# A Trainium2 transformer block: three of four row blocks turned by DMA, residual sums shared by VectorE and GpSimd, a small product moved to VectorE, and a new order

## The chip, the cores and the metric

One Trainium2 core runs the whole program. TensorE (PE) multiplies, VectorE (DVE), ScalarE (ACT) and GpSimd (POOL) do the elementwise work, and SyncE (SP) issues every DMA transfer, one after the other in a written order. The metric is the device time of one execution in microseconds; lower is better. Before the change it is 191.43 us, the median of three runs (191.26 to 191.53).

## What is computed

```python
def _A_ref(x, wqkv, wo):                  # B, S, D = 1, 2048, 448; H = 16 heads of 28
    qkv = (x @ wqkv).reshape(B, S, 3, H, Dh) ...
    off = jnp.arange(8) * 2               # each row looks at itself and 7 rows before it, two apart
    logits = jnp.einsum("bhsd,bhswd->bhsw", q, kg) * scale
    attn = _softmax(jnp.where(mask, logits, -1e9))
    o = jnp.einsum("bhsw,bhswd->bhsd", attn, vg)
    return o...reshape(B, S, D) @ wo

def _B_ref(x, w1, w2, w3, w4):
    h = _gelu(_layernorm(x) @ w1)         # 448 to 448
    hs = concat(four groups of 112 channels, shifted by 1, -1, 2, -2 rows) @ w2
    x1 = x + hs
    return x1 + _gelu(_layernorm(x1) @ w3) @ w4     # 448 to 1792 to 448

h  = x + _A_ref(_layernorm(x), wqkv, wo)
h2 = h + _B_ref(_layernorm(h), w1, w2, w3, w4)
```

Inputs, weights and output are bfloat16.

## The kernel before

The 2048 rows stand in 16 tiles of 128 rows (`xin`), four tiles to a block. Blocks t = 0 to 3 go through these phases: N1 (statistics and normalise into `lntm`), A1 (turn the normalised rows so that features lie on partitions, `actT`, then q and k), V, A2 (scores: products `qk_r` of q with eight shifted copies of k on VectorE, summed over a head's features on TensorE with the 0/1 matrix `zc`), S (softmax: `mx`, `ls`, `pb`, turned on TensorE to `pt`), A3 (`bd_r`: probabilities spread into block-diagonal form on VectorE, then multiplied with `vw`, the windowed values), O (the product with `wo_s`, and the residual sum into `xin`), B1 and M (norm, turn, w1 and gelu into `gT`). The second half runs in five units of 2, 4, 4, 4 and 2 tiles: B2 (w2, then `xb` = residual + product, f32), T (norm of `xb`, and the outer residual `xb += xin`), W3 (gelu into `h3T`), B3 (w4, the last sum into `ost`, and the store). In the profile the large buffers share one allocation and show as `arena`: an `arena<-arena,xin` row on 128x448 f32 is the outer residual sum `xb += xin`; `arena<-xin,rs_y,ps` is the eviction of w2 into `xb`; `lntm<-arena,...` the norm of unit T.

Every operation is recorded first by `_Sched.add` or `group`, with its reads and writes, and given a number. The engines' programs are then cut from one list, `ORDER` (line 22 on): each engine runs its operations in the order in which their numbers stand there, and so does SP with its transfers. Buffers are handed out in that order too (`arrange`), and semaphore waits are derived from it (`_emit_plan`). Nothing is decided while the kernel runs. An operation that may run on either of two engines has an alternative in `alts`; the numbers in `OTHER` (line 53) take it. All operations are issued from one line of `emit_engine`, 1011 before and 1012 after, so the rows of the profile are told apart by the names of their tiles; line 1006 is a load of ScalarE's function table.

`TURN` (line 13) says for each block and phase how `transposed` turns the normalised rows: `t` by TensorE transposes and two copies out of PSUM, `d` by one DMA transpose that SP issues. Block 0 of A1 with `t` takes `transposed_single`. For `d`, `normalize` writes 512 columns per tile (two overlapping pieces of 256) in place of 448. The matmuls of this kernel contract 64 rows at a time, so that two run beside each other in the two halves of TensorE (`duo`); that is why rows read `64*128 64x448`.

`rstd` computes the reciprocal deviation; for the norm B1 (kind 1) it also makes `mrs`, the mean times the reciprocal deviation, that the last sum in B3 adds. `phase_B2` issues the 16 outer residual sums on GpSimd.

Of the kernel before, what the change touches and what calls it, by code (L numbers as in the profile page):

```python
# [6 lines left out]
ALU = mybir.AluOpType  # L7
# [2 lines left out]
F32 = mybir.dt.float32  # L10

_LAST = {}
TURN = {'A1': 'ttdd', 'B1': 'dddd', 'B2': 'ddddd'}
NORM = {'N0': 'vvvv', 'N1': 'avvv', 'B1': 'avvv', 'B2': 'avvvv'}
STATS = {'N1': 'vvva', 'B1': 'avaa', 'B2': 'avvvv'}
NBD, NLN, NACT, NSM, NO = 3, 2, 4, 1, 5
# [3 lines left out]
STAGE = '....'  # L20
ALONE = False
ORDER = """
# [29 lines left out]
"""  # L52
OTHER = """
91 94 114 187 188 501 507 549 550
"""
FULL = (4,)
FILL = (1, 1, 0, 0)
# [228 lines left out]
def bass_sequential_preLN__sliding_local_dilated__mixer_s_mlp__prompt_kernel(  # L286
# [16 lines left out]
    S = _Sched()  # L303
# [16 lines left out]
    with ExitStack() as es:  # L320
# [3 lines left out]
        xin = sb("xin", [128, NTL, D], BF16)  # L324
# [17 lines left out]
        rs_y = sb("rs_y", [128, 3, 2, NTL], F32)  # L342
        mrs = sb("mrs", [128, NTL], F32)
        nm = sb("nm", [128, 3, NTL], F32)
# [35 lines left out]
        xb = [arv(A_KV + i // 4 * KVB, 128, 4 * D * 2).bitcast(F32).rearrange("p (i d) -> p i d", d=D)[:, i % 4, :] for i in range(NTL)]  # L380
# [28 lines left out]
        def dve(meth, block=False, **kw):  # L409
            op = S.add("dve", meth, **kw)  # L410
            op.block = block
            return op

        def pool(meth, **kw):
            return S.add("pool", meth, **kw)
# [90 lines left out]
        def rstd(kind, i, m=4, summed=False, norms="v", how="p"):  # L506
            var = mv[:, kind, i:i + m, 1]
            by = 1.0 / D if summed else 1.0
            first = int(kind == 1)
            shifted_ = "a" in norms  # L510

            def power(k):
                S.add("pool", "tensor_tensor", out=rs_y[:, kind, k, i:i + m], in0=rs_x[:, kind, k, i:i + m], in1=mhalf[:, 0:m], op=ALU.pow)

            def power_act(k):
                act(rs_x[:, kind, k, i:i + m], var, ACT.Ln, scale=by * (1.0 + EPS * k), bias=epsilon[:, k:k + 1])
                act(rs_y[:, kind, k, i:i + m], rs_x[:, kind, k, i:i + m], ACT.Exp, scale=-0.5)

            def shift(k):
                if m == 1:  # L520
                    act(nmr[:, kind, i:i + 1], nm[:, kind, i:i + 1], ACT.Identity, scale=rs_y[:, kind, k, i:i + 1])
                else:
                    dve("tensor_tensor", out=nmr[:, kind, i:i + m], in0=nm[:, kind, i:i + m], in1=rs_y[:, kind, k, i:i + m], op=ALU.mult)

            if not summed and (shifted_ or kind == 1):
                dve("tensor_scalar", out=nm[:, kind, i:i + m], in0=mv[:, kind, i:i + m, 0], scalar1=-1.0, scalar2=None, op0=ALU.mult)
            if how == "a":
                power_act(first)
                if shifted_:
                    shift(first)  # L530
                if kind == 1:
                    power_act(0)
            else:
                if kind == 1:
                    dve("tensor_scalar", out=rs_x[:, kind, 1, i:i + m], in0=var, scalar1=by * (1.0 + EPS), scalar2=EPS * EPS, op0=ALU.mult, op1=ALU.add)
                    power(1)
                    if shifted_:
                        shift(1)
                if kind == 1 or summed:
                    dve("tensor_scalar", out=rs_x[:, kind, 0, i:i + m], in0=var, scalar1=by, scalar2=EPS, op0=ALU.mult, op1=ALU.add)  # L540
                else:
                    dve("tensor_scalar", out=rs_x[:, kind, 0, i:i + m], in0=var, scalar1=EPS, scalar2=None, op0=ALU.add)
                power(0)
                if kind != 1 and shifted_:
                    shift(0)
            if kind == 1:
                pool("tensor_tensor", out=mrs[:, i:i + m], in0=nm[:, 1, i:i + m], in1=rs_y[:, 1, 0, i:i + m], op=ALU.mult)

        CHUNK = (0, 128, 192, 320)

# [111 lines left out]
        def phase_N1(t):  # L662
            ln = a1_ln[t] = _Tile(P_ln)
            summed = STATS["N1"][t] == "a"
            for lo, step in FIRST if t == 0 else ((4 * t, 4),):
# [9 lines left out]
                for n, i in enumerate(range(lo, lo + step)):  # L675
                    normalize(0, i, ln, i % 4, xin[:, i, :], TURN["A1"][t], summed, norms[n])

        def phase_A1(t):
            a = a1_a[t] = transposed(a1_ln[t], TURN["A1"][t]) if t or TURN["A1"][t] == "d" else transposed_single(a1_ln[t])
            now = 2 + t * 512  # L680
# [171 lines left out]
        def phase_B1(t):  # L852
# [9 lines left out]
            for n, i in enumerate(range(4 * t, 4 * t + 4)):  # L862
                normalize(1, i, ln, n, xin[:, i, :], TURN["B1"][t], summed, norms[n])
            a = transposed(ln, TURN["B1"][t])
            S.tag = "M%d" % t
# [22 lines left out]
        def phase_B2(u):  # L888
# [28 lines left out]
            for n, i in enumerate(tiles):  # L917
                normalize(2, i, ln, n, xb[i], TURN["B2"][u], summed, norms[n])
            for i in tiles:
                S.add("pool", "tensor_tensor", out=xb[i], in0=xb[i], in1=xin[:, i, :], op=ALU.add).block = True  # L920
            b2_a[u] = transposed(ln, TURN["B2"][u], len(tiles))

        h3 = {}
# [129 lines left out]
```

## Time and profile before

| what | value |
|---|---|
| median of three runs | 191.43 us |
| profiled execution, its own time | 191.99 us |
| its span on the core | 190.3 us |
| granted TensorE clock | 1.00 |
| TensorE busy | 180.0 us, 95% |
| VectorE busy | 129.9 us, 68% |
| ScalarE busy | 123.4 us, 65% |
| GpSimd busy | 26.5 us, 14% |

The span is what the trace covers; 1.69 us of the execution lie around it. Busy time of matmuls is modelled at its end, and consecutive matmuls overlap a little, so a loss is better read from start to start than from the idle time alone. VectorE's 68% is an average: it is nearly always busy in the first half of the span, and seldom in the second.

### The profile page before, as it was taken

The page shows a single profiled execution, that of the slowest core. Times are in us where ns is not written, and L with a number is a line of the kernel's source. Part 1 is how long each engine was busy: PE and PEld are TensorE (multiplying, and loading weights), DVE is VectorE, ACT ScalarE, POOL GpSimd, SP SyncE. Part 2 cuts the span into 40 slices and gives each one's busy share as a digit, 9 for nine tenths or more (in the row PEclk, how much of TensorE's full clock was granted, in tenths as well). Part 3 has the DMA queues.
Part 4 walks back from the last instruction along what each step waited for, and adds up shares of the span by engine and source line. Part 5 has one row for each costly group of instructions (what it writes and reads, how often), then busy time and mean ns, then how long its engine had stood idle before and what let it go on. Part 6 is the DMA issues. An engine that isn't in the chain of part 4 may idle for free.

```text
span 190.3 us, 5623 instructions
## 1 busy us (share of the span) xinstructions
PE 180.0 (95%) x2434; PEld 96.3 (51%) x2434; DVE 129.9 (68%) x226; ACT 123.4 (65%) x282; POOL 26.5 (14%) x61
## 2 busy tenths in 40 slices
PE   6699999897999989999989999999999999999994
PEld 2496433354443545565645535545444454455672
DVE  6999999999999999998998940099850006002203
ACT  3459999998999999999644897910256303650250
POOL 2250000000010000002205100181386002000000
DMA  5950254477407895796250060015044004000031
GB/s 147 339 193 3 44 110 110 78 174 158 103 3 114 160 272 225 136 331 134 50 113 0 5 134 0 3 30 108 0 91 119 0 0 112 19 3 0 17 109 48
DMA packets 36577, 18.06 MB, mean 95 GB/s; under 512 B 25304, under 2 KB 36040, under 8 KB 36552
## 3 DMA queue, kind: packets, MB, share of 16 engines
q1 hardware_dynamic: 36552, 17.70, 38.3%
q8 instruction: 19, 0.31, 0.7%
q14 instruction: 6, 0.05, 0.1%
HBM read 7.91 MB, written 1.84 MB: 51 GB/s over the span
## 4 chain that ended last, share of the span: by engine, by line
PE 56%; DVE 22%; ACT 11%; DMA 5%; SPq 2%; issue 2%; DVEq 0%; ACTq 0%
PE ps L1011 56%; DVE qk_r L1011 6%; DVE lntm L1011 5%; DVE bd_r L1011 4%; DMA arena<-in_A_wqkv_dram 3%; ACT lntm L1011 3%; SPq L1011 2%; DMA wo_s<-in_A_wo_dram 2%; ACT arena L1011 2%; DVE arena L1011 1%; ACT xin L1011 1%; DVE mx L1011 1%; DVE st L1011 1%; ACT h3T L1011 1%; ACT rs_x L1011 1%
## 5 line engine op out<-in xcount | busy, mean ns | idle before, releaser
L1011 PE MATMUL ps<-actT,arena 64*128 64x512 bf16 (+1 forms) x756 | 69.4, 329 | 0.9 <-ACT h3T L1011 0.4
L1011 ACT ACTIVATE h3T<-ps 128x512 bf16<-128x512 f32 (+1 forms) x70 | 30.8, 518 | 41.2 <-PE ps L1011 41.0
L1011 PEld LDWEIGHTS ps<-actT,arena 64*128 64x128 bf16 x756 | 37.3, 94 | 28.5 <-PE ps L1011 2.1
L1011 PE MATMUL ps<-arena,h3T 64*128 64x448 bf16 (+2 forms) x434 | 44.9, 343 | 0.4 <-DVE arena L1011 0.3
L1011 DVE SCALAR_TENSOR_TENSOR ost<-ps,mrs,arena 128x448 bf16<-128x448 f32 (+1 forms) x17 | 10.8, 650 | 40.6 <-PE ps L1011 40.6
L1011 ACT ACTIVATE arena<-ps 128x512 bf16<-128x512 f32 (+3 forms) x63 | 31.5, 541 | 3.7 <-PE ps L1011 3.2
L1011 PEld LDWEIGHTS ps<-arena,h3T 64*128 64x128 bf16 (+1 forms) x434 | 22.9, 94 | 20.0 <-DVE arena L1011 0.7
L1011 DVE TENSOR_TENSOR qk_r<-arena 128x4096 bf16<-128x4096 bf16 (+1 forms) x16 | 32.0, 2013 | 0.3 <-PE ps L1011 0.3
L1011 DVE TENSOR_TENSOR bd_r<-arena,bmask 80x2048 bf16<-80x2048 bf16 x16 | 19.8, 1270 | 0.1
L1011 POOL TENSOR_TENSOR arena<-arena,xin 128x448 f32<-128x448 f32 x16 | 17.1, 1086 | 14.8 <-DVE lntm L1011 14.8
L1011 DVE TENSOR_SCALAR lntm<-arena,mv,rs_y 128x512 bf16<-128x512 f32 x14 | 8.9, 679 | 12.2 <-ACT rs_y L1011 11.7
L1011 PE MATMUL ps<-wo_s,actT 64*128 64x448 bf16 x128 | 14.8, 350 | 1.1 <-DMA wo_s<-in_A_wo_dram 1.0
L1011 PE MATMUL ps<-w_s,arena 64*128 64x448 bf16 (+1 forms) x128 | 14.2, 350 | 0.1
L1011 PE MATMUL ps<-actT,w_s 64*112 64x512 bf16 x112 | 13.4, 378 | 0.0
L1011 ACT ACTIVATE actT<-ps 128x512 bf16<-128x512 f32 (+2 forms) x18 | 11.2, 653 | 3.2 <-PE ps L1011 3.2
L1011 PE MATMUL ps<-arena,actT 64*128 64x448 bf16 x112 | 13.2, 350 | 0.1
L1011 ACT ACTIVATE lntm<-xin,nm 128x448 bf16<-128x448 bf16 x16 | 10.5, 662 | 3.6 <-DVE nm L1011 3.6
L1011 POOL TENSOR_TENSOR mrs<-nm,rs_y 128x4 f32<-128x4 f32 x4 | 1.5, 387 | 71.9 <-ACT rs_y L1011 70.1
L1011 DVE SCALAR_TENSOR_TENSOR arena<-xin,rs_y,ps 128x448 f32<-128x448 bf16 x16 | 10.4, 667 | 0.0
L1011 DVE BATCH_NORM_STATS2 st<-xin 128x6 f32<-128x448 bf16 x16 | 9.2, 611 | 0.9 <-DMA xin<-in_A_x_dram 0.9
L1011 PEld LDWEIGHTS ps<-wo_s,actT 64*128 64x128 bf16 x128 | 5.6, 94 | 7.6 <-PE ps L1011 1.5
L1011 PEld LDWEIGHTS ps<-actT,w_s 64*112 64x112 bf16 x112 | 7.0, 127 | 4.7 <-DMA actT<-lntm 0.4
(70 smaller groups left out, 158.0 us busy)
## 6 DMA issues: line engine op xcount, KB each, us to landing
arena<-in_B_w_dram SPq DMA_DIRECT2D x2, 896.0 KB, 6.5
out_dram<-ost SPq DMA_DIRECT2D x15, 112.0 KB, 2.0
arena<-in_B_w_dram SPq DMA_DIRECT2D x2, 784.0 KB, 5.7
vw<-vt SPq DMA_DIRECT2D x4, 320.0 KB, 3.8
vw<-vt SPq DMA_DIRECT2D x4, 256.0 KB, 3.6
arena<-in_A_wqkv_dram SPq DMA_DIRECT2D x2, 448.0 KB, 4.7
xin<-in_A_x_dram SPq DMA_DIRECT2D x2, 448.0 KB, 7.2
xin<-in_A_x_dram SPq DMA_DIRECT2D x3, 224.0 KB, 5.9
```

The lines of the kernel that those rows point to most:

```text
L1011: inst = getattr(eng, meth)(**kw)
```

## The change

Four things differ. `TURN['A1']` becomes `tddd`: block 1, too, is turned by one DMA transpose. The product `mrs` goes from GpSimd to VectorE. The 16 outer residual sums get VectorE as their alternative (the mark `block` that they lose is read nowhere). `ORDER` is a new list (853 operations for 858, since block 1's 4 transpose groups and 2 copies become one transfer), and `OTHER` names other operations: nine of the sixteen sums (546, 607, 608, 609, 679, 680, 681, 750, 811), the q/k copies 88 and 96, three norms of block 1 of B1 (186, 187, 189), and, as before, the two evictions of the last attention block and two norms of unit 0.

```diff
-TURN = {'A1': 'ttdd', 'B1': 'dddd', 'B2': 'ddddd'}
+TURN = {'A1': 'tddd', 'B1': 'dddd', 'B2': 'ddddd'}
...
 ORDER = """
-29 0 6 7 1 2 30 31 8 48 49 50 51 9 53 54 52 11 10 60 61 58 59 32 55 56 57 62 63 64 65 39 40 41 42 43 44 45 46 47 87 89
+2 0 1 6 29 5 30 7 31 4 8 48 49 9 53 54 50 51 52 55 56 10 60 58 59 61 57 32 39 40 41 42 43 44 45 46 87 47 88 62 63 65
...
 OTHER = """
-91 94 114 187 188 501 507 549 550
+88 96 186 187 189 496 502 544 545 546 607 608 609 679 680 681 750 811
 """
...
             if kind == 1:
-                pool("tensor_tensor", out=mrs[:, i:i + m], in0=nm[:, 1, i:i + m], in1=rs_y[:, 1, 0, i:i + m], op=ALU.mult)
+                dve("tensor_tensor", out=mrs[:, i:i + m], in0=nm[:, 1, i:i + m], in1=rs_y[:, 1, 0, i:i + m], op=ALU.mult)
...
             for i in tiles:
-                S.add("pool", "tensor_tensor", out=xb[i], in0=xb[i], in1=xin[:, i, :], op=ALU.add).block = True
+                both = dict(out=xb[i], in0=xb[i], in1=xin[:, i, :], op=ALU.add)
+                S.add("pool", "tensor_tensor", alts=[("dve", [("tensor_tensor", both)])], **both)
             b2_a[u] = transposed(ln, TURN["B2"][u], len(tiles))
```

The first place is SP's queue behind the loads of x, near the start: `lntm` to `actT` is a turn, `arena` to `arena` are the halo copies of k, `vt` to `vw` the windowed values. Before:

```order
L1011 DMA xin<-in_A_x_dram 128x4x448 x2
L1011 DMA arena<-arena 128x3x16
L1011 DMA arena<-arena 64x4x16
L1011 DMA arena<-arena 64x3x16
L1011 DMA arena<-arena 64x16
L1011 DMA_TRANSPOSE actT<-lntm 128x16x128
```

After:

```order
L1012 DMA xin<-in_A_x_dram 128x4x448 x2
L1012 DMA_TRANSPOSE actT<-lntm 128x16x128
L1012 DMA arena<-arena 64x4x16
L1012 DMA arena<-arena 64x3x16
L1012 DMA arena<-arena 128x3x16
L1012 DMA vw<-vt 64x4x512
L1012 DMA_TRANSPOSE actT<-lntm 128x16x128
```

Before, the one turn in this piece is block 2's; after, the first is block 1's and the second block 2's, with three halo copies and one transfer of values between them.

The second place is TensorE from the softmax of the last block to the w3 product of unit 2 (`ident,pb`: turn of the probabilities; `actT,w_s` and `w_s,arena`: w1 and w2; `arena,h3T`: w4; `actT,arena`: w3). Before:

```order
L1011 MATMUL ps<-ident,pb 80x64 x16
L1011 MATMUL ps<-actT,w_s 112x512 x28
L1011 MATMUL ps<-arena,h3T 128x448 x14
L1011 MATMUL ps<-bd_r,vw 32x64 x96
L1011 MATMUL ps<-w_s,arena 128x448 x8
L1011 MATMUL ps<-wo_s,actT 128x448 x8
L1011 MATMUL ps<-bd_r,vw 32x64 x32
L1011 MATMUL ps<-wo_s,actT 128x448 x16
L1011 MATMUL ps<-w_s,arena 128x448 x8
L1011 MATMUL ps<-wo_s,actT 128x448 x8
L1011 MATMUL ps<-actT,arena 128x512 x8
```

After:

```order
L1012 MATMUL ps<-ident,pb 80x64 x16
L1012 MATMUL ps<-arena,h3T 128x448 x14
L1012 MATMUL ps<-actT,w_s 112x512 x22
L1012 MATMUL ps<-bd_r,vw 32x64 x64
L1012 MATMUL ps<-actT,w_s 112x512 x6
L1012 MATMUL ps<-wo_s,actT 128x448 x8
L1012 MATMUL ps<-bd_r,vw 32x64 x64
L1012 MATMUL ps<-wo_s,actT 128x448 x16
L1012 MATMUL ps<-w_s,arena 128x448 x8
L1012 MATMUL ps<-wo_s,actT 128x448 x8
L1012 MATMUL ps<-w_s,arena 128x448 x24
L1012 MATMUL ps<-actT,arena 128x512 x98
```

The w4 group went ahead of w1, the last six w1 matmuls went behind the first half of the `bd_r` groups, which are now two and two in place of three and one, and the w3 product of unit 2 runs in one piece behind all of w2, where two pieces of it stood between w2 groups before.

The third place is VectorE at the same time (`pb`: probabilities; `lntm<-arena`: norms of unit 1; `xin,mv<-ps,xin`: residual sum behind wo). Before:

```order
L1011 TENSOR_TENSOR pb<-ls,mx 128x8x64
L1011 TENSOR_SCALAR lntm<-arena,mv,rs_y 128x512 x2
L1011 TENSOR_SCALAR nm<-mv 128x4
L1011 TENSOR_SCALAR lntm<-arena,mv,rs_y 128x512
L1011 TENSOR_TENSOR bd_r<-arena,bmask 80x2048 x2
L1011 TENSOR_SCALAR lntm<-arena,mv,rs_y 128x512
L1011 TENSOR_TENSOR bd_r<-arena,bmask 80x2048
L1011 CAST actT<-ps 128x512
L1011 TENSOR_TENSOR bd_r<-arena,bmask 80x2048
```

After:

```order
L1012 TENSOR_TENSOR pb<-ls,mx 128x8x64
L1012 TENSOR_SCALAR lntm<-arena,mv,rs_y 128x512 x3
L1012 TENSOR_TENSOR mrs<-nm,rs_y 128x4
L1012 TENSOR_TENSOR bd_r<-arena,bmask 80x2048 x3
L1012 CAST actT<-ps 128x512
L1012 TENSOR_TENSOR bd_r<-arena,bmask 80x2048
L1012 TENSOR_SCALAR lntm<-arena,mv,rs_y 128x512
L1012 CAST actT<-ps 128x512
L1012 SCALAR_TENSOR_TENSOR ost<-ps,mrs,arena 128x448
L1012 SCALAR_TENSOR_TENSOR xin,mv<-ps,xin 128x448
L1012 TENSOR_TENSOR arena<-arena,xin 128x448
```

The fourth norm of unit 1 went behind the last `bd_r`, `mrs` stands where `nm` stood, and the first of the moved residual sums stands between two of the sums behind wo.

56 rows, old and new, of the table ORDER are left out of this document.

## The prediction

> **What bounds the kernel now.** I read the busy time by stretches of the span first, then the waits of TensorE, then the chain of waits, and last the instructions that took longer than their like.
>
> ```profile
> 8.50:44.00 35.50, 33.73 (x555) 19.06 (x555) 34.87 (x52) 31.83 (x79) 3.80 (x26) 1.00 0.48 112
> 44.00:63.00 19.00, 18.35 (x324) 8.26 (x326) 18.47 (x27) 17.85 (x50) 0.73 (x1) 1.00 0.47 93
> 63.00:90.00 27.00, 26.17 (x430) 14.92 (x426) 26.36 (x48) 26.02 (x57) 0.86 (x1) 1.00 0.81 212
> 90.00:112.00 22.00, 21.04 (x328) 11.45 (x328) 20.06 (x39) 14.10 (x29) 4.80 (x8) 1.00 0.23 47
> 112.00:134.00 22.00, 21.70 (x220) 11.10 (x220) 10.56 (x20) 10.71 (x20) 5.33 (x6) 1.00 0.25 53
> 134.00:191.00 57.00, 53.68 (x566) 29.11 (x562) 13.00 (x25) 19.38 (x42) 9.54 (x9) 1.00 0.17 43
> ```
>
> Behind each stretch stand its length and the busy time of TensorE (matmul, then weight load), VectorE, ScalarE and GpSimd, then the granted clock, 1.00 throughout. There are two regimes. From 8.5 to 90 us VectorE is busy 79.70 of 81.5 us: there it paces, and TensorE runs just behind it. From 112 us VectorE is busy less than half of the time and TensorE alone is full. So an idle moment of TensorE before 90 us is mostly VectorE's arrears, and if it is removed it comes back elsewhere; one behind 90 us lengthens the kernel.
>
> The waits of TensorE behind 90 us (start, duration, and in brackets the idle time and what ended it), with a few rows beside them that run undisturbed:
>
> ```profile
> 96.03 0.70 PE L1011 MATMUL ps<-bd_r,vw 80*32 80x64 bf16 x64
> 97.30 0.42 PE L1011 MATMUL ps<-bd_r,vw 80*32 80x64 bf16 x32 [0.56 <-DVE bd_r L1011]
> ...
> 106.14 4.51 PE L1011 MATMUL ps<-actT,arena 64*128 64x512 bf16 x40
> 111.05 1.04 PE L1011 MATMUL ps<-actT,arena 64*128 64x512 bf16 x8 [0.40 <-ACT h3T L1011]
> ...
> 123.12 1.49 PE L1011 MATMUL ps<-arena,h3T 64*128 64x448 bf16 x14
> 124.44 1.68 PE L1011 MATMUL ps<-w_s,arena 64*128 64x448 bf16 x16
> 125.96 1.50 PE L1011 MATMUL ps<-arena,h3T 64*128 64x448 bf16 x14
> 127.75 6.79 PE L1011 MATMUL ps<-arena,h3T 64*128 64x448 bf16 x70 [0.29 <-DVE arena L1011]
> 134.38 13.98 PE L1011 MATMUL ps<-actT,arena 64*128 64x512 bf16 x128
> 148.20 5.46 PE L1011 MATMUL ps<-arena,h3T 64*128 64x448 bf16 x56
> ```
>
> Matmuls overlap at their ends, so I price a wait from start to start. 128 matmuls of 512 columns take 148.20 - 134.38 = 13.82 us undisturbed, 0.108 each; 14 of 448 take 124.44 - 123.12 = 1.32. The two groups at 96.03 take 1.27 where 0.70 is their whole duration: 0.57 lost on bd_r. The 40 from 106.14 take 4.91 against 4.32: 0.59 on the gelu output h3T. The 14 from 125.96 take 1.79 against 1.32: 0.47 on the w2 eviction. Together 1.63 us.
>
> Who was late stands in the chain of waits (start, duration, engine, what it writes):
>
> ```profile
> 92.40 3.25 DVE bd_r L1011 x2
> ...
> 104.34 0.95 DVE nm L1011
> ...
> 123.34 3.17 DVE lntm L1011 x4
> ```
>
> Each is VectorE work that took longer than its like, as the tiles' rows say (ns: least, median, most), and at each of the three times a residual sum runs on GpSimd:
>
> ```profile
> L1011 DVE TENSOR_TENSOR bd_r<-arena,bmask x16: 1209/1214/2109, 36.9 to 97.8; 80x2048 bf16<-80x2048 bf16 x16
> L1011 DVE TENSOR_SCALAR lntm<-arena,mv,rs_y x14: 533/538/1264, 90.9 to 157.6; 128x512 bf16<-128x512 f32 x14
> L1011 DVE TENSOR_SCALAR nm<-mv x6: 159/170/944, 27.4 to 104.3; 128x4 f32<-128x4 f32 x5, 128x2 f32<-128x2 f32 x1
> ```
>
> ```profile
> 92.40 1.03 POOL L1011 TENSOR_TENSOR arena<-arena,xin 128x448 f32<-128x448 f32 x1
> ...
> 102.24 3.02 POOL L1011 TENSOR_TENSOR arena<-arena,xin 128x448 f32<-128x448 f32 x3
> ...
> 123.11 2.21 POOL L1011 TENSOR_TENSOR arena<-arena,xin 128x448 f32<-128x448 f32 x2
> ```
>
> The worst case lies 0.90, 0.73 and 0.77 us over the median. The first pair starts in the same instant, 92.40; the third sum of the second row ends at 105.26 and the held nm at 105.29; the four norms take 3.17 us where 4 x 0.538 = 2.15 would do. VectorE is held until the sum of GpSimd is over.
>
> **The change, part by part.**
>
> *Residual sums.* Nine of sixteen go to VectorE, the other seven keep GpSimd and stand elsewhere in its order. VectorE's price for an f32 sum of 128x448 is not in the trace. From below: the f32 norm above, 538 ns for 512 columns with one tensor input, 0.47 us. From above, a product of two f32 tensors:
>
> ```profile
> L1011 DVE TENSOR_TENSOR pb<-ls,mx x4: 657/680/691, 35.0 to 90.3; 128x512 bf16<-128x512 f32 x4
> ```
>
> 0.680 / 512 x 448 = 0.60 us. I take 0.60, the form being the nearer: 5.4 us for nine. One of them stands between the xin sums of block 3, at some 101 us, where VectorE has 22.00 - 20.06 = 1.94 us free in 22; the others come behind block 3's norm, where it has 11.4 us free up to 134 and 44 behind. So 0.60 lies on a dense stretch; I charge 0.2 of it, a third, since TensorE has w2 matmuls to run there.
>
> The gain: without a GpSimd sum at 92.40 the bd_r chain is 0.90 us earlier, more than the wait of 0.57. The nm is 0.78 us earlier (0.95 less 0.17), and with it the squares, the table load and the gelu behind it: more than 0.59. The four norms are 1.02 earlier, more than 0.47. So the waits end, and the gain is their 1.63, not the 2.7 by which VectorE is earlier. It hangs on cover: in the new order of TensorE, 14 matmuls of the w4 product now stand ahead of w1 and 24 of w2 ahead of the 98 of w3. If that cover is gone, bd_r's 0.57 stays.
>
> The Trainium skill, page "SBUF — State Buffer", section "Who interferes with whom", has a rule for these rows: VectorE and GpSimd share a pair of ports as an exclusive lock, and a VectorE instruction with two SBUF inputs contends with a GpSimd instruction that reads SBUF. The 2109 against 1214 ns of bd_r agree. By this rule the moved sums, each with two inputs in SBUF, stand in the lock too, whenever one of the seven others runs.
>
> *The small product mrs*, four times on VectorE, is priced by nm above, 0.17 us: 0.7 in all, two of the four on the dense stretches. I charge 0.1. Below that it can be nothing, above it 0.34.
>
> *Block 1 turned by one transfer.*
>
> ```profile
> 13.86 0.65 PE L1011 MATMUL ps<-ident,lntm 64*128 64x64 bf16 x32
> 14.33 0.75 PE L1011 MATMUL ps<-arena,actT 64*128 64x448 bf16 x6
> ...
> 16.98 3.97 PE L1011 MATMUL ps<-actT,arena 64*128 64x512 bf16 x42
> ```
>
> ```profile
> 14.27 7.09 SPq L1011 DMA_DIRECT2D arena<-arena  x4
> 21.62 1.80 SPq L1011 DMA_TRANSPOSE actT<-lntm  x1
> ```
>
> ```profile
> DMA to landing us min/median/max: 3.1/4.3/6.7
> ```
>
> TensorE loses 32 transposes (14.33 - 13.86 = 0.47 us) and ScalarE their two copies; SP gains one transfer. The rows are normalised by 13.86, so it lands at 13.86 + 4.3 = 18.2, with bounds of 17.0 and 20.6. TensorE reaches block 1's q and k at 16.98 today; the new order puts 16 score matmuls of 512 columns ahead (16 x 0.108 = 1.7) and takes the 0.47 out: 18.2. It arrives as it is wanted; at the far bound TensorE stands 2.4 us. I charge nothing and credit nothing: the products of VectorE pace this stretch, and block 1's are queued behind those of block 0. What is late next is SP: its queue is in order, so block 0's halo copies come behind the turn, and block 2's turn, at 21.62 today, behind them.
>
> *The wo weights* feel that last:
>
> ```profile
> 44.11 0.93 PE L1011 MATMUL ps<-wo_s,actT 64*128 64x448 bf16 x8 [0.95 <-DMA wo_s<-in_A_wo_dram]
> ```
>
> SP's new order has copies that wait for ScalarE between the four loads; I put the last some 1.7 us later (an added turn of 1.8 us). TensorE has 14 more matmuls of 512 columns ahead of the projection, 1.5 us. The wait goes from 0.95 to 1.15; its bounds are nothing and 2.65. I charge 0.1, half of the 0.2, since VectorE paces.
>
> *The rest of the two tables.* Evictions and norms trade places between ScalarE and VectorE in equal numbers but one, 0.54 us of VectorE by the f32 norm above, at the end where it is free. Nothing.
>
> **The sum.** -1.63 + 0.2 + 0.1 + 0.1 = -1.23 us. I add -0.2 for the gelu that starts 0.78 us earlier and lets the following w4 groups follow closer: -1.4. The profiled execution took 191.99 us (span 190.3, and 1.69 around it), 0.56 above the median of the runs; a change of 1.4 is the same for both, so against the median 191.43 - 1.4 = **190.0 us**.
>
> **The rivals.**
>
> *Front debt, slower (chance 0.24).* Block 1's transfer lands at its far bound, block 2's turn and the wo loads move with it, and TensorE owes more than VectorE's pace hides. For: four small copies took 7.09 us of SP's time, so its queue stalls readily. Against: VectorE is full up to 90 us and would have to go idle first. It decides once block 1 lands later than about 19. Price: at 20.6, the 2.4 of block 1 less the 0.8 that VectorE is ahead by (81.5 - 79.70 = 1.80 us of free time in the stretches, about half of it here), 1.6, and 0.7 at wo, less the 1.4: 192.3.
>
> *The waits only move (0.12).* VectorE's 0.60 + 0.34 on dense stretches, and the new order, set the same waits at other instructions. For: 1.94 us of free time in 90 to 112. Against: the three holds by GpSimd were 2.7 us. 191.4.
>
> *The lock again (0.08).* The seven sums left on GpSimd meet bd_r and nm, or VectorE's own sums, at up to 1.03 us each: the waits of 0.57 and 0.59 stay, 0.47 goes, 191.0. For: seven chances. Against: in the order the first stands beside xin sums that read PSUM, the second behind the last bd_r, the others behind block 3's norm, where VectorE is free. The rule of "SBUF — State Buffer" in the Trainium skill is this rival's.
>
> *More (0.08).* TensorE keeps the 0.47 of the transposes and the 0.95 of wo as well: 190.0 - 1.4 = 188.6.
>
> **How the numbers follow.** The forecast has 0.48; its own range is 189.0 to 190.9, from a gain of 2.4 (VectorE's 2.7 nearly whole) to one of 0.5 (one wait of three). Less than 0.2%, 0.38 us, can hardly be told from no change. Faster: 0.48 + 0.08 + 0.06 of the lock's 0.08 = 0.62. Same: 0.12. Slower: 0.24 and the 0.02 left of the lock. The range, 188.4 to 192.4, holds the case of more and most of the front debt.
>
> **What would show it.** Right: behind 90 us no wait of TensorE above 0.2 us on bd_r, h3T or the w2 eviction; no bd_r above 1.3 us; block 1 landing before 18.5; a wait on wo below 1.3. Wrong: TensorE waiting on actT's transfer between 18 and 32 us, a wait on wo above 1.6, or a bd_r, an nm or a sum of VectorE of a microsecond beside a sum of GpSimd.

## The result: a gain of 0.7 us, and the profile after

The changed kernel takes 190.76 us (median of 20 runs, 190.20 to 191.62), the kernel before 191.45 us (20 runs, 190.90 to 191.88): the ratio is 0.997, with a 95% interval of 0.9957 to 0.9982. The forecast of 190.0 us had the direction and more than twice the size. The profiled execution took 190.65 us, with a span of 188.6 us; that of before had 191.99 and 190.3. So the span shrank by 1.7 us between the two, the median by 0.69.

The busy time of the changed kernel by stretches, in the columns of the same view of before:

```profile
44.00:63.00 19.00, 17.49 (x318) 8.09 (x316) 18.89 (x30) 18.41 (x51) 0.00 (x0) 1.00 0.43 92
63.00:90.00 27.00, 26.07 (x418) 15.13 (x418) 26.02 (x48) 25.29 (x56) 2.12 (x2) 1.00 0.73 198
90.00:112.00 22.00, 21.93 (x340) 12.50 (x342) 18.93 (x40) 15.84 (x32) 1.20 (x2) 1.00 0.44 66
112.00:134.00 22.00, 22.00 (x228) 14.26 (x225) 12.39 (x27) 8.85 (x17) 0.00 (x0) 1.00 0.20 44
```

From 90 to 134 us TensorE is busy 43.93 of 44 us, where it was 42.74: no wait is left there. From 44 to 63 us it is busy 17.49 us, where it was 18.35. The chain of waits of the changed kernel, from the DMA turn of block 0's second norm to the end, says the first in another way:

```profile
57.19 5.95 DMA actT<-lntm
...
63.18 2.60 PE ps L1012 x22
...
65.80 2.07 ACT arena L1012 x4
...
68.00 10.06 PE ps L1012 x132
...
96.98 88.33 PE ps L1012 x967
185.31 0.03 issue
185.33 1.12 DVE ost L1012 x2
```

The three links of before through bd_r, nm and the f32 norms are gone. From 68.00 us the chain is TensorE alone (the rows left out are `issue` of up to 0.14 us and TensorE), up to the last two sums; ahead of that stand the turn, the first w1 matmuls and their gelu on ScalarE, and no VectorE. In time, the start of the w4 product of unit 0 (x42) and the last 42 matmuls of the changed kernel, from the timeline of TensorE:

```profile
87.08 4.45 PE L1012 MATMUL ps<-arena,h3T 64*128 64x448 bf16 x42
...
180.46 5.50 PE L1012 MATMUL ps<-arena,h3T 128*128 128x224 bf16 x42
```

and of the kernel before:

```profile
87.06 4.38 PE L1011 MATMUL ps<-arena,h3T 64*128 64x448 bf16 x42
...
182.17 5.50 PE L1011 MATMUL ps<-arena,h3T 128*128 128x448 bf16 x42
```

From the first row to the end of the second are 98.88 us now and 100.61 before: 1.73 us less. The first row stands at the same time in both. What the profile after shows ahead of it is a wait that before did not have (the DMA turn, 0.71 us):

```profile
61.98 0.49 PE L1012 MATMUL ps<-ident,pb 64*80 64x64 bf16 x16 [0.45 <-DVE pb L1012]
63.18 3.23 PE L1012 MATMUL ps<-actT,w_s 64*112 64x512 bf16 x28 [0.71 <-DMA actT<-lntm]
```

The same place in the kernel before:

```profile
62.70 0.46 PE L1011 MATMUL ps<-ident,pb 64*80 64x64 bf16 x16
63.00 3.21 PE L1011 MATMUL ps<-actT,w_s 64*112 64x512 bf16 x28
```

The first w1 product (block 0) starts 1.20 us behind the turns of the probabilities, where it was 0.30 before: it waits for the DMA turn of block 0's second norm. The instructions of VectorE that the forecast speaks of:

```profile
L1012 DVE TENSOR_TENSOR bd_r<-arena,bmask x16: 1208/1211/1222, 36.6 to 96.6; 80x2048 bf16<-80x2048 bf16 x16
L1012 DVE TENSOR_SCALAR lntm<-arena,mv,rs_y x14: 527/542/1259, 90.9 to 154.6; 128x512 bf16<-128x512 f32 x14
L1012 DVE TENSOR_TENSOR arena<-arena,xin x9: 595/618/1337, 100.1 to 155.1; 128x448 f32<-128x448 f32 x9
...
L1012 DVE TENSOR_SCALAR nm<-mv x6: 154/170/170, 22.5 to 103.1; 128x4 f32<-128x4 f32 x5, 128x2 f32<-128x2 f32 x1
```

No bd_r and no nm is held any more. Two f32 norms (1259 and 1257 ns, at 139.2 and 140.4 us) and one moved sum (1337 ns, at 155.1 us) still are, beside sums that stayed on GpSimd, the first three of them here and two more at 154.73 us:

```profile
138.90 3.63 POOL L1012 TENSOR_TENSOR arena<-arena,xin 128x448 f32<-128x448 f32 x3 [0.66 <-DVE lntm L1012]
```

TensorE shows no wait above 0.2 us behind 90 us, so these holds cost it nothing.

### The profile page after: what moved, and what is told of

Its sections match the earlier page's. It is cut to its first block, busy times and chain, and to the rows that moved or that the text cites. A ratio compares the mean times of both kernels' runs of the same rounds, so it can differ in the third digit from the quotient of the medians.

```text
span 188.6 us, 5558 instructions
## 1 busy us (share of the span) xinstructions
PE 180.1 (95%) x2402; PEld 106.2 (56%) x2402; DVE 133.3 (71%) x239; ACT 121.4 (64%) x280; POOL 16.9 (9%) x48
## 4 chain that ended last, share of the span: by engine, by line
PE 66%; DVE 19%; ACT 8%; DMA 4%; issue 1%; DVEq 0%
PE ps L1012 66%; DVE qk_r L1012 8%; ACT arena L1012 5%; DVE bd_r L1012 4%; DMA actT<-lntm 3%; DVE lntm L1012 2%; ACT lntm L1012 2%; DVE mx L1012 1%; DVE st L1012 1%; DMA xin<-in_A_x_dram 1%; ACT vt L1012 1%; DVE pb L1012 1%; DVE ls L1012 1%; DVE ost L1012 1%; DVE mv L1012 0%
## 5 line engine op out<-in xcount | busy, mean ns | idle before, releaser
L1012 PE MATMUL ps<-actT,arena 64*128 64x512 bf16 (+1 forms) x756 | 67.9, 329 | 0.3 <-issue 0.2
L1012 PEld LDWEIGHTS ps<-actT,arena 64*128 64x128 bf16 x756 | 41.4, 94 | 23.6 <-PE ps L1012 1.8
L1012 PEld LDWEIGHTS ps<-arena,h3T 64*128 64x128 bf16 (+1 forms) x434 | 28.1, 95 | 14.3 <-PE ps L1012 0.5
L1012 DVE TENSOR_TENSOR bd_r<-arena,bmask 80x2048 bf16<-80x2048 bf16 x16 | 18.9, 1212 | 0.3 <-PE ps L1012 0.2
L1012 POOL TENSOR_TENSOR arena<-arena,xin 128x448 f32<-128x448 f32 x7 | 8.6, 1239 | 72.3 <-DVE lntm L1012 72.3
L1012 PE MATMUL ps<-arena,actT 64*128 64x448 bf16 x112 | 12.7, 351 | 0.3 <-DMA actT<-lntm 0.2
L1012 ACT ACTIVATE actT<-ps 128x512 bf16<-128x512 f32 (+1 forms) x16 | 9.2, 609 | 1.9 <-PE ps L1012 1.8
L1012 PEld LDWEIGHTS ps<-actT,w_s 64*112 64x112 bf16 x112 | 7.5, 127 | 4.9 <-DMA actT<-lntm 0.8
L1012 PEld LDWEIGHTS ps<-w_s,arena 64*128 64x128 bf16 (+1 forms) x128 | 6.8, 95 | 5.7 <-issue 0.7
L1012 DVE TENSOR_SCALAR lntm<-arena,mv,rs_y 128x512 bf16<-128x512 f32 x14 | 8.4, 643 | 2.0 <-POOL rs_y L1012 2.0
```

The costliest lines, as they stand in the source:

```text
L1012: inst = getattr(eng, meth)(**kw)
```

## The experiments

Each was compared with the kernel before on the same chip. "Around" is a run's own time less its span, as a median over its runs. The ratio is not the quotient of the two medians (for e2 that would be 0.997, where the means of the runs give 0.9951).

| run | median us | ratio to before, 95% | span | around |
|---|---|---|---|---|
| e1, before again | 191.40 | 1.0001 (0.9982 to 1.0021) | 189.7 | 1.73 |
| e2, e14, e16, the change again | 190.71, 189.89, 190.73 | 0.9949, 0.9922, 0.9949 | 188.65, 187.85, 188.7 | 2.03, 2.05, 2.05 |
| e3, before, nine sums on VectorE | 192.97 | 1.0072 (1.0051 to 1.0094) | 190.9 | 2.01 |
| e4, the change, all sums on GpSimd | 190.64 | 0.9960 (0.9942 to 0.9978) | 188.9 | 1.78 |
| e5, e15, front of before, late order of the change | 190.24, 190.13 | 0.9933, 0.9939 | 188.5, 188.35 | 1.72, 1.75 |
| e6, small vw transfers ahead of the turn | 190.30 | 0.9933 (0.9914 to 0.9953) | 188.3 | 1.99 |
| e7, before, turn ahead of the loads | 200.17 | 1.0449 (1.0411 to 1.0486) | 198.45 | 1.75 |
| e8, the change, block 1 turned by TensorE | 192.22 | 1.0037 (1.0014 to 1.0060) | 190.2 | 2.03 |
| e9, the change, GpSimd's program padded | 190.33 | 0.9944 (0.9922 to 0.9966) | 188.55 | 1.72 |
| e10, e13, large vw transfer behind the turn | 190.69, 190.93 | 0.9955, 0.9953 | 188.65, 188.85 | 2.02, 2.03 |
| e11, before, turn behind the loads | 192.77 | 1.0071 (1.0050 to 1.0092) | 191.05 | 1.73 |
| e12, e10 with all sums on GpSimd | 190.17 | 0.9933 (0.9908 to 0.9958) | 188.45 | 1.75 |

### Before and after once more (e1, e2)

Nothing is edited.

> The kernel before once more, nothing changed, for a second profile and the span of each run. Theory (the shown execution of before was an untypical one): its own time less its span comes out near 2.0 us, as in the changed kernel's runs (190.65 against 188.6), and the median span lies near 189.4, so that the gain of the spans is about 0.7 us and the waits behind 90 us add up to clearly less than 1.63. Rival (the waits are as shown in every run): the span is 189.8 to 190.0, the time around it 1.5 to 1.7, and the same three waits stand in the profile with 1.63 us together; then 0.3 us of the gain is lost outside of the span.

> The changed kernel once more, nothing changed. Both theories: ratio 0.996 to 0.998, no wait of TensorE above 0.2 us behind 90 us. If its spread (190.2 to 191.6) comes from the transfers of the front, the place where the second half starts (the w4 run at 87.08 us) moves with the span by up to a microsecond; if not, the span moves behind it.

The waits of the kernel before, in its second profile:

```profile
96.61 0.42 PE L1011 MATMUL ps<-bd_r,vw 80*32 80x64 bf16 x32 [0.56 <-DVE bd_r L1011]
110.36 4.82 PE L1011 MATMUL ps<-actT,arena 64*128 64x512 bf16 x42 [0.40 <-ACT h3T L1011]
127.06 6.79 PE L1011 MATMUL ps<-arena,h3T 64*128 64x448 bf16 x70 [0.30 <-DVE arena L1011]
```

They are the same three, 0.56, 0.40 and 0.30 us, only 0.69 us earlier: this part of the profile is the same in both executions, and the shown execution had been late at the front. From unit 0's w4 to the end of TensorE e1 takes 100.62 us again, e2 98.90. The rival for e1 was right up to its margins: the waits stand in full and 1.73 us lie around the span, where it had 1.5 to 1.7; the median span, 189.7 us, lies between the two expectations (189.4 and 189.8). The 12 runs of e1 and 26 of the kernel beside it all lie between 1.67 and 1.81 us around the span, those of e2 between 1.95 and 2.12. So 0.3 us of the changed kernel lie outside of the span.

### The sums without the order, the order without the sums (e3, e4)

```diff
 OTHER = """                                   (e3, in the kernel before; phase_B2 as in the change)
-91 94 114 187 188 501 507 549 550
+91 94 114 187 188 501 507 549 550 551 612 613 614 684 685 686 755 816
...
 OTHER = """                                   (e4, in the changed kernel)
-88 96 186 187 189 496 502 544 545 546 607 608 609 679 680 681 750 811
+88 96 186 187 189 496 502 544 545
```

> The order of before, with the same nine residual sums on VectorE as in the change. Theory (the holds by GpSimd make the late waits, and the order only keeps clear of them): the sum that stands beside bd_r at 92.40 stays on GpSimd, so its wait of 0.57 stays; nm is held by one sum in place of three, and the four norms at 123 are free: 0.5 to 1.0 us faster than before. Rival (the order alone makes the gain): within 0.3 us of before.

> The changed kernel with all sixteen residual sums on GpSimd in the new order. Theory: 0.4 to 1.2 us slower than the changed kernel, with a bd_r, nm or f32 norm held beside a sum. Rival (the order alone): within 0.2 us of the changed kernel, so 190.6 to 190.9.

e3 is 0.7% slower than before, e4 as fast as the change. In e3 two of the three waits are gone, as its theory had it: nm takes 0.17 us and the four norms 1.92, and only the wait on bd_r stays, with 0.51 us. But in the order of before, VectorE meets five of the moved sums in a row, and the last sums of B3 (`ost`) and the norms behind them are late; VectorE and then TensorE of e3:

```profile
127.39 2.74 DVE L1012 TENSOR_TENSOR arena<-arena,xin 128x448 f32<-128x448 f32 x5
```

```profile
136.04 4.82 PE L1012 MATMUL ps<-actT,arena 64*128 64x512 bf16 x42 [0.65 <-DVE ost L1012]
141.22 4.06 PE L1012 MATMUL ps<-actT,arena 64*128 64x512 bf16 x36 [0.37 <-DVE ost L1012]
```

These and a third wait on ost, 0.26 us at 159.80, are new: 1.28 us, more than the two waits saved. And e4, the new order with every sum on GpSimd, has no bd_r that is held:

```profile
L1012 DVE TENSOR_TENSOR bd_r<-arena,bmask x16: 1210/1216/1222, 36.2 to 96.5; 80x2048 bf16<-80x2048 bf16 x16
```

```profile
98.26 2.03 POOL L1012 TENSOR_TENSOR arena<-arena,xin 128x448 f32<-128x448 f32 x2 [8.13 <-DVE lntm L1012]
```

The new order puts the sums behind the last bd_r (96.5 us and 1.2), on whichever engine. From unit 0's w4 on, e4 takes 98.88 us, as the change does. So the late gain is the order's, and in this order the move to VectorE adds nothing to it. For e4 that is the rival theory, number included. For e3 both numbers were wrong: it was to be 0.5 to 1.0 us faster or within 0.3 us of before, and is 1.6 us slower.

### Block 1's turn alone (e7, e11, e8)

```diff
-TURN = {'A1': 'ttdd', ...                     (e7 and e11, in the kernel before)
+TURN = {'A1': 'tddd', ...
-... 212 209 213 214 211 215 216 217 218 ...
+... 212 209 211 213 ...                       (e7; the loads 18 and 19 stand further back)
+... 212 209 211 18 19 213 ...                 (e11)
...
-TURN = {'A1': 'tddd', ...                     (e8, in the changed kernel)
+TURN = {'A1': 'ttdd', ...
```

> The kernel before with block 1 turned by one transfer, issued right behind the loads of x, and nothing else moved. Theory (the turn of block 1 is hidden and its cost in the change lies elsewhere): within 0.3 us of before, TensorE waits for block 1's actT under 0.5 us, the wo wait up to 0.5 longer. Rival (front debt): a wait on block 1 of over a microsecond and 192.0 us or more.

> The kernel before with block 1 turned by one transfer, this time behind the loads of x for blocks 2 and 3 in SP's queue; the earlier try had it ahead of them, and VectorE stood 6.9 us for x. Theory (the turn alone costs little where the queue is kept free): 191.2 to 192.2 us, a wait of under 0.7 on block 1's actT. Rival (front debt: in this order the turn comes too late for TensorE): a wait of over a microsecond on it and over 192.3 us.

> The changed kernel with block 1 turned again by TensorE, the transposes between q, k and v of block 0, and two copies of a microsecond each on ScalarE there. Theory (the DMA turn is neutral): within 0.3 us of the change, the wait on block 0's second turn unchanged at 0.7. Rival (the DMA turn is what makes the front of the change later): 0.4 to 0.8 faster than the change.

In e7 the turn stood ahead of two loads of x in SP's queue. SP and VectorE of e7:

```profile
13.24 2.09 SPq L1011 DMA_TRANSPOSE actT<-lntm  x1
15.38 1.50 SPq L1011 DMA_DIRECT2D xin<-in_A_x_dram  x2
```

```profile
20.09 0.63 DVE L1011 BATCH_NORM_STATS2 st<-xin 128x6 f32<-128x448 bf16 x1 [6.88 <-DMA xin<-in_A_x_dram]
```

SP waits for the norm that the turn reads, the loads wait behind it, and VectorE stands 6.88 us for x. e7 is 8.7 us slower than before, and 7.4 slower than e11, which differs from it by the place of these two loads alone; e7's theory had 0.3 us at most. Not all of that is waiting: the clock granted to TensorE was 0.82 from 21 to 40 us of e7's profile and 1.00 in its other stretches. With the loads ahead, in e11, TensorE waits for the turn:

```profile
17.62 1.69 PE L1011 MATMUL ps<-actT,arena 64*128 64x512 bf16 x14 [1.12 <-DMA actT<-lntm]
```

and the kernel is 1.4 us slower than before, as the rival for e11 had it. The front of before has no work to put there. The changed order has, and reaches block 1 at 18.61 us, when its transfer (issued at 13.59, 4.4 us to landing) has been there since 17.99. In e8, TensorE's turn in the changed order costs 1.5 us, where the theory had 0.3 at most and the rival a gain. ScalarE's two copies (1.94 us from 14.39 us) stand between its copies out of PSUM into `arena`, and TensorE waits for the first of the two:

```profile
15.47 2.49 PE L1012 MATMUL ps<-arena,actT 64*128 64x448 bf16 x22 [1.12 <-ACT actT L1012]
```

Its place was one choice of several, so 1.5 is an upper bound. The turn is worth 1.4 us one way in one order and at most 1.5 the other way in the other: a turn and its order can't be priced apart.

### The turn that w1 waits for (e6, e10, e13, e14, e16)

```diff
-... 24 360 25 190 467 195 ...  361 ...        (190: block 0's second turn; 467, 361: small vw transfers; 360: the large one)
+... 24 360 25 467 361 190 195 ...             (e6)
+... 24 25 467 361 190 360 195 ...             (e10, e13)
```

> The changed kernel with two small vw transfers issued ahead of block 0's second turn (the one that w1 of block 0 waits for), into a stretch where SP's queue is idle, in place of right behind it. Theory (they share the engines of the turn and make it land 5.9 to 6.0 us after its issue, 4.8 to 5.0 in before): it lands after 4.8 to 5.2, w1's first matmul starts within 0.4 us of the turns of the probabilities, and the time falls by 0.5 to 0.8 us, to about 190.1. Rival (it lands late for another reason, such as its place in the queue or its buffer): 5.9 again, 190.5 to 190.9.

> The changed kernel with the two small vw transfers ahead of block 0's second turn and a large one of 320 KB right behind it, as in before. Theory (how the turn ends depends on what the queue is given next; behind a large transfer it landed 4.4 to 5.0 us after its issue): it lands after 4.4 to 5.2, w1 follows the turns of the probabilities without a wait, 0.5 to 0.8 us faster than the change. Rival (the lateness is the turn's own in this order): 5.9 to 6.1 again and no gain.

> The changed kernel with the large vw transfer behind the turn, once more, beside the changed kernel on the same chip. Theory: the turn lands after 4.4 to 5.2 us again and the median is 0.4 to 0.7 us below that of the changed kernel. Rival (it lands late in some runs of both): the median is within 0.2 us of it, and both have runs near 187.7 and near 188.7 us of span.

> The changed kernel a third time, to be set against the run before it on the same chip. Theory: the turn lands after 5.9 to 6.1 us, spans mostly 188.5 to 189.0. Rival: it lands early in this profile, with a span near 187.7.

> The changed kernel a fourth time, beside the run before it. Both: 2.0 around the span, 98.9 us from unit 0's w4 to the end of TensorE. Theory: the span goes with the landing of block 0's second turn, near 187.6 at 4.6 to 4.8 us, 188.4 to 188.9 at 5.9 to 6.1; the median of the runs near 190.6.

In e6 the turn landed 6.1 us after its issue, so sharing the DMA engines with the two small transfers behind it isn't the cause. e6's median, 190.30, lies between its two expectations. In e10 it landed after 4.8 us, w1 did not wait, and the execution was the shortest of its eight, 189.64; but the median was that of the change. e13, the same kernel, landed after 6.1 us and e14, the change itself, after 4.6. The landing is not decided by what stands behind the turn. Of e13 and e14, on one chip, the change has the lower median by 1.0 us, with six runs; neither of e13's expectations had that. The view of the tile actT in the changed kernel's first profile, and in e14, the issue in question alone:

```profile
L1012 SPq DMA_TRANSPOSE actT<-lntm x1: 2061/2061/2061, 57.2 to 57.2; - x1
...
DMA to landing us min/median/max: 5.9/5.9/5.9
```

```profile
L1012 SPq DMA_TRANSPOSE actT<-lntm x1: 2037/2037/2037, 56.8 to 56.8; - x1
...
DMA to landing us min/median/max: 4.6/4.6/4.6
```

and TensorE in e14:

```profile
61.54 0.49 PE L1012 MATMUL ps<-ident,pb 64*80 64x64 bf16 x16 [0.46 <-DVE pb L1012]
61.87 3.21 PE L1012 MATMUL ps<-actT,w_s 64*112 64x512 bf16 x28
...
66.49 0.42 PE L1012 MATMUL ps<-bd_r,vw 80*32 80x64 bf16 x32 [0.72 <-DVE bd_r L1012]
```

The same program, the same issue, 1.3 us apart in landing; the spans are 188.6 and 187.6. In ten profiles of kernels with the changed front it landed eight times after 5.9 to 6.1 us and twice (e10, e14) after 4.6 and 4.8. In the eight others (before, e1, e3, e5, e7, e8, e11, e15) it landed after 4.4 to 5.0 each time. So the rival held for the edit of e10: no gain at the median, and a late landing again in e13. The late landing was seen in kernels with the changed front alone. What in that front makes it late stays open. Block 1's DMA turn in the old order (e7, e11) and the new order without it (e8) both landed early, but these are three profiles, and two of ten landed early with both. Nor is a late landing itself new: in the kernel before the next turn, of block 1 at 63.92 us, landed 6.7 us after its issue, and 6.6 in e1, where TensorE did not wait for it.

### The time around the span (e9)

```diff
+        pad = sb("pad", [128, 8], F32)
...
+        for _ in range(9):
+            S.add("pool", "memset", ap=pad[:], constant=0.0)
         order = S.arrange(...)                (853 to 861 at the end of ORDER)
```

> The changed kernel with nine small memsets of an unused tile at the end of GpSimd's program, where it has nothing left to do, so that it is again as long as in before. Theory (the 0.3 us that the changed kernel has more around its span hang on the length of GpSimd's program, which shows as 5 instruction transfers on queue q14 in place of 6): 6 transfers, the time less the span goes from 2.03 to 1.75 us, the span stays at 188.4 to 188.9, and the time falls by 0.3. Rival (it hangs on VectorE's longer program, or on chance): 5 or 6 transfers, but 2.0 around the span.

The row of queue q14 on the pages of the change and of e9; the page of before has that of e9:

```profile
q14 instruction: 5, 0.04, 0.1%
```

```profile
q14 instruction: 6, 0.05, 0.1%
```

With nine memsets that nobody reads the sixth transfer is back, the time around the span is 1.72 us in place of 2.03, and the median 190.33. Over all kernels run here the two go together: 6 transfers with 1.71 to 1.78 us (before, e1, e4, e5, e7, e9, e11, e12, e15), 5 with 1.99 to 2.05 (the change, e3, e6, e8, e10, e13). Moving nine sums off GpSimd shortened its program, and that cost 0.3 us where no engine's row shows it. How the length acts is open.

### Versions meant to beat both (e5, e12, e15)

e5 and e15 take the first 472 operations of the old order but one (to the norms of unit 0, at 75 us), then the rest in the new one, with all sums on GpSimd and mrs on VectorE. e12 is e10 with all sums on GpSimd.

> The order of before up to unit 0's norms (472 operations, to about 75 us, block 1 turned by TensorE), then the rest in the order of the change; all sums on GpSimd, mrs on VectorE. Theory (the late order gains 1.73 us by itself, the front of the change loses 0.5 to 1.0, and the moved sums add 0.27 around the span): from the start of q and k to unit 0's w4 78.4 us as in before, from there to the end of TensorE 98.9 as in the change, 1.75 around the span: 189.5 to 189.9 us. Rival (the late gain needs the change's front): 98.9 grows to 100 or more, 190.6 to 191.4.

> The order of the change with the large vw transfer behind block 0's second turn and all sixteen sums on GpSimd: a version that should beat both. Theory (the two losses add: 0.5 to 0.6 us at the turn, 0.3 around the span): 6 instruction transfers on q14, 1.75 around the span, 78.1 us from q and k to unit 0's w4, 98.9 behind it: 189.6 to 190.2. Rival (the turn's landing varies from run to run, whatever stands behind it): 190.3 to 190.6, only the 0.3 of the time around the span.

> The front of before with the late order of the change, once more, beside the changed kernel on one chip. Theory (in the order of before the turn that w1 of block 0 waits for lands after 4.8 to 5.0 us every time): 4.8 to 5.0 again, no wait at w1, 1.75 around the span, 0.3 to 0.7 us below the changed kernel's median. Rival (its landing is chance here too): 5.9 to 6.1, and no more than 0.3 below.

TensorE of e5, at the two places from which the late stretch is read:

```profile
86.66 4.45 PE L1011 MATMUL ps<-arena,h3T 64*128 64x448 bf16 x42
...
180.05 5.50 PE L1011 MATMUL ps<-arena,h3T 128*128 128x224 bf16 x42
```

98.89 us on the front of before: the late gain needs nothing of the new front. The medians are 190.24 and 190.13 us, e5's above the 189.5 to 189.9 that were expected; beside e15, on the same chip, the change (e16) took 190.73. In e15 the turn landed after 4.8 us, but unit 0's w4 waited 0.62 us for the load of its weights, so the late stretch took 99.63 us there. In e12's profile the turn landed late (6.1 us, and 79.42 from q and k to unit 0's w4, where its theory had 78.1); its median of 190.17 is within the theory's range all the same. The three versions are 1.2 to 1.4 us faster than before at the median. Against the change on the same chip, e15 is 0.60 us faster (e16) and e12 is 0.28 slower (e14, six runs), so e12 has not been shown to beat it. For e15, the intervals against before, 0.9918 to 0.9959 for e15 and 0.9928 to 0.9969 for e16, overlap, so that e15 beats the change is likely and not sure.

## Why the forecast was right in direction and too large

**The late waits: right, and nearly the sum as well.** Forecast were waits of 1.63 us and 0.2 beyond, less 0.2 for the sum on the dense stretch and 0.1 for mrs, 1.53 in all; 1.73 us are gone in the profile of the change, 1.72 in e2's against e1's, and no wait above 0.2 us is left behind 90 us. Which VectorE instructions held them, and beside what, was read rightly: in e3, where one sum stays beside bd_r, a bd_r takes 2051 ns again.

**"Sums off GpSimd": half of the reason fell.** The prices were good, 0.618 us measured for a sum against 0.60, 0.150 for mrs against 0.17. But e4 has the whole late gain with all sums on GpSimd. In the new order the holds are ended by the order, not by the engine. The rival of the lock came in part: two norms and one moved sum still meet a sum on GpSimd, the sum with 1337 ns, which the forecast had named as a sign of being wrong. It cost nothing here, since they meet at 139 to 142 us and at 155, where TensorE does not wait for them.

**The step that failed: the front was charged 0.1.** The forecast read the stretch from 63 to 90 us as paced by VectorE, since it is busy 26.36 of 27 us there, and concluded that a late TensorE comes back. The same row has TensorE busy 26.17 of 27: both are full. In the chain of before VectorE does stand up to 97 us, but the change takes these waits away, and in its profile VectorE has no link in the chain from 57.19 us up to the last two sums; the late turn, w1, the gelu and then TensorE alone pace. So most of what is late at w1 stays late to the end. From the first w1 product to unit 0's w4 the kernel before takes 24.06 us (63.00 to 87.06). The change takes 24.21 where the turn landed early (e14, 61.87 to 86.08, with the 0.72 us for bd_r in it) and 23.90 where it landed late (63.18 to 87.08): of the 0.96 us by which w1 starts later in e16 than in e14, some 0.3 come back.

The transfer of block 1, which the forecast worked out, was hidden as it said (landed 17.99, wanted 18.61). The second turn of block 0, which SP issues 44 us later, got no term, and in eight of ten profiles it is the one that lands 5.9 to 6.1 us after its issue, against 4.8 in before. From the start of q and k to unit 0's w4 those eight take 78.92 us on the average, the two others 78.08, and the five with the front of before and no edit of the turn (before, e1, e3, e5, e15) 78.41. The change loses 0.5 us in the first case and gains 0.3 in the second. Some 0.65 of the 0.84 us between the two is the turn's, by e14 and e16. The wait on wo, up to 0.73 us in the eight and none in the two, may be the rest; no run separates it.

**A term that was missing: the time around the span.** "A change of 1.4 is the same for both" took it as fixed. It grew by 0.3 us, with GpSimd's shorter program.

**The sum again**: -1.73 late, +0.34 at the front (eight of ten at +0.51, two at -0.33), +0.31 around: -1.08 us, where the medians give -0.62 to -0.72 in the three comparisons with 12 and 20 runs (by their ratios -0.6 to -1.0), and -1.64 in e14 with six. The remaining 0.4 of the medians isn't located: the start of q and k alone varies between 7.99 and 8.54 us over these profiles, and the profiles are few. How often the turn lands early can be guessed from the spans. Of the 50 runs of the change (the result's, e2, e14, e16) seven have 187.5 or 187.6 us and all others 188.1 to 189.6; the two profiles with an early landing have 187.6 and 187.7. If the short spans are the early landings, which is not shown, they are one in seven, and none of the result's 20 runs: there the front counts with +0.51 and the sum is -0.91.

**The front rival** (block 1's transfer late, then wo; 192.3 us) named the right part of the kernel and the wrong transfer. wo became better than forecast: the wait of 0.95 us is 0 to 0.38 in nine of the ten profiles with the changed front and 0.73 in e12. TensorE has 14 matmuls more ahead of it, as was worked out; that these alone make the wait shorter is not shown. That rival's mechanism is real in the old order, as e11 shows with 1.4 us.

## What to carry to other kernels

A stretch in which one engine is full is paced by it only if the other is not full as well: read both columns, and ask what paces once the change has taken its waits away, before a late start is written off as recovered, and follow every transfer that a changed queue issues, not only the one that is added. An operation that holds another by a shared resource may be moved in time as well as to another engine; here the order brought the whole late gain, and the move of nine sums cost 0.3 us around the span. And a difference of profiles is not a difference of medians: look at the time around the span and at a second profile of the same program before a term of half a microsecond is believed.

## What the runs showed of the hardware that was not expected

The time of an execution outside of its span goes with the length of GpSimd's program: 1.71 to 1.78 us with six instruction transfers on q14, 1.99 to 2.05 with five, and nine idle memsets moved one kernel from the second to the first. One and the same DMA transpose, block 0's second turn, lands 4.4 to 5.0 or 5.9 to 6.1 us after its issue over 18 profiles, with nothing between; the changed program has both, 4.6 and 5.9 to 6.1, in four executions. The turn behind it has other values, 5.2 in the change and 6.7 in before. A DMA transpose ahead of two loads in a queue, waiting for its input, made the kernel 7.4 us slower than the same transpose behind them. In that kernel (e7) the granted TensorE clock was 0.82 from 21 to 40 us, with TensorE busy 14.56 of 19 us, and 0.982 or 0.983 over each of its six runs.
